# GEGLU block: sums of the down weights on GpSimd, and another order of the opening

## Chip, cores and metric

The kernel runs on one core of a Trainium2 chip. The metric is the device time of one execution in microseconds. Three runs of the kernel before took 549.56 to 552.13 us, with a median of 549.72 us.

## What is computed

The reference, cut to what matters (x is 2048 x 1024, the gate and up weights 1024 x 3584, the down weights 3584 x 1024, all bf16):

```python
def reference(x, w_gate, w_up, w_down):
    g = jnp.einsum("bsd,df->bsf", x, w_gate)
    u = jnp.einsum("bsd,df->bsf", x, w_up)
    h = _gelu(g) * u
    return jnp.einsum("bsf,fd->bsd", h, w_down)
```

## The kernel before

All three products are made by a Winograd form of Strassen's scheme: a product of 2 x 2 blocks by seven block products in place of eight, at the price of sums of blocks that are made ahead. Here `s` are sums of weight blocks and `t` sums of blocks of x; the products that use them run on TensorE in fp32r.

**Passes and units.** The 2048 rows are taken in two passes (`ip`) of 1024 rows, each as two blocks of 512 columns of the transposed x (`xT[0]`, `xT[1]`). In a pass, 14 units (`u`) each make 256 columns of h from 256 columns of both weights; then the down stage (`down`) makes the output of the pass.

**One unit** (`unit`). TensorE issues, in this order: the product of the weights' second half with `xT[0]`; s2 with t2; s1 with t1; s3 with t3; s4 with tb; the first product of the next unit (`ahead_of_p4`); sa with t4. Each of these is done for gate and up. ACT copies intermediate results out of PSUM (`snap`) and makes the gelu; VectorE adds them (`add`, `new`) and multiplies into `hT` (`times`). The last unit has no next unit's product.

**What stands beside a unit.** `prepare` runs after the s1 product has been issued. It lets GpSimd make the eight s sums of the next unit (`make_s(ahead, pool)`), has SP load the weights of the unit after the next (`load_w`, two DMAs of 512 KB, three buffers `w`), and has SP fetch the raw down weights that the next unit will need (`fetch_wd`, two DMAs of 256 KB for each j). `aside(-1)` of unit 1 issues the load of unit 2's weights on ACT's queue.

**The sums of the down weights.** For each of 14 block rows j (`NJ`) the down stage needs three sums of blocks of the down weights. The first pass makes them once and keeps them in DRAM (`td`), where the down stage of both passes loads them (`load12`, `load4`). Each j is a set: `keep(j, part)` makes one of three tensor_tensor sums on VectorE, in the tile `m` (one buffer), at the points `aside(0)`, `aside(1)`, `aside(2)` of a unit; `store_made(j)` has SP store the tile of 768 KB. `making(u)` says which j a unit makes: one each in units 2 to 12, two in units 6, 8 and 10, none in unit 13. The store of a unit's last set is issued at the head of the next unit's program.

**The down stage.** Step -1 to 2 of `down` has SP load the raw weights of the first product (`fetch12`, L305, 256 KB each; one serves two steps of four products), and after them the sums from DRAM (L266, L273). TensorE's first product of the stage reads the first of these tiles.

**The opening.** Some 8 products of zeros (`NWARM`, L460) run while x is loaded. `turn` transposes a block of x on TensorE, four tiles of 128 rows, and copies each from PSUM (L424 VectorE, L426 ACT, by turns). Unit 0 is done with plain products (`plain`): first block of x, transposed; the first half of its products; second block transposed; the second half; then the products of the second block. Its weights come in eight DMAs of 128 KB (L433). VectorE makes the s of unit 1 and the t sums of the pass in between.

**What sets the order.** SP, VectorE, GpSimd and TensorE execute in the order in which the program issues (`manual_schedule(engines=ORDER)`); ACT has its order from a scheduler, apart from the opening. Small tiles (s, t, raw, copies) share 52 slots of 2 KB per partition (`slot`); a tile gets a slot when an earlier one is released.

Helpers record most operations: L90 is every tensor_tensor on VectorE, L93 every one on GpSimd, L111 every product, L107 the copies out of PSUM, L243 the fetch of raw down weights, L256 the store of the sums, L121 the load of unit weights.

Of the kernel before, what the change touches and what calls it, by code (L numbers as in the profile page):

```python
# [10 lines left out]
def kernel(  # L11
# [23 lines left out]
    nc = tc.nc  # L35
    ENG = mybir.EngineType
    ORDER = {ENG.SP, ENG.DVE, ENG.Pool, ENG.PE}
    P = nc.NUM_PARTITIONS
    bf16 = mybir.dt.bfloat16
# [15 lines left out]
    N = 512  # L55
    NS = N // P
    NPASS = S // (2 * N)
    NU = NFB // 2
    NWARM = 8
    SLOTS = 52  # L60
    LAG = 3
    BIG12 = (0, 2, 4)
# [26 lines left out]
    def dve(out, a, b, op):  # L89
        nc.vector.tensor_tensor(out=out, in0=a, in1=b, op=op)  # L90
# [85 lines left out]
    def gelu(src):  # L176
        g = slot([P, N], f32, "g")
        nc.scalar.activation(g, src, ACT.Gelu_apprx_tanh)  # L178
        return g

    def times(fb, c, g, u):
        dve(hT[:, fb // NJ, fb % NJ, c, :], g, u, MUL)

    def product(ps, lhs, rhs, start):
        for k in range(KH):
            matmul(ps, lhs[:, k, :], rhs[k], start and k == 0, k == KH - 1)
# [6 lines left out]
    def unit(u, banks, xT, w, s, t, p1, after_p5, aside, ahead_of_p4):  # L193
        GU = range(2)

        def add(ps, other):

            g = new(dve, ps[0], other[0], ADD, "sum", dtype=f32)
            dve(ps[1], ps[1], other[1], ADD)
            return g, ps[1]  # L200

        b21 = [xT[0][:, KH + k, :] for k in range(KH)]
        e, c, d = banks
        aside(-1)
        for i in GU:
            product(c[i], w[:, i, KH:, :P], b21, True)
        g, up = add(c, p1)
        for i in GU:
            product(e[i], s["s2"][i], t["t2"], False)
        times(2 * u, 0, gelu(g), up)  # L210
        aside(0)
        u2 = [snap(e[i], "u2") for i in GU]
        c = d
        for i in GU:
            product(c[i], s["s1"][i], t["t1"], True)
        p5 = [snap(c[i], "p5") for i in GU]
        after_p5()
        for i in GU:
            product(e[i], s["s3"][i], t["t3"], False)
        g, up = new(dve, e[0], p5[0], ADD, "sum", dtype=f32), banks[1][1]  # L220
        dve(up, e[1], p5[1], ADD)
        for i in GU:
            product(c[i], s["s4"][i], t["tb"], False)
        times(2 * u + 1, 1, gelu(g), up)
        aside(1)
        g, up = add(c, u2)
        ahead_of_p4()
        for i in GU:
            product(e[i], s["sa"][i], t["t4"], False)
        times(2 * u, 1, gelu(g), up)  # L230
        aside(2)
        times(2 * u + 1, 0, gelu(e[0]), e[1])
# [9 lines left out]
        for kh in range(2):  # L242
            nc.sync.dma_start(out=wraw[j][kh], in_=wdn[:, kh, j, :])  # L243

    def keep(j, part):
        ra, rb = wraw[j]
        if part == 0:
            made[j] = mpool.tile([P, 3, N], f32r, name="m")
            dve(made[j][:, 0], ra[:, N:], ra[:, :N], SUB)
        elif part == 1:  # L250
            dve(made[j][:, 1], rb[:, N:], made[j][:, 0], SUB)
        else:
            dve(made[j][:, 2], rb[:, :N], made[j][:, 1], SUB)

    def store_made(j):
        nc.sync.dma_start(out=td[:, j], in_=made[j].bitcast(f32))  # L256

    q12, s12, q73, q4, raw = {}, {}, {}, {}, {}  # L260

# [152 lines left out]
            t.append(xn)  # L414
        return t

    def turn(xT, xn, c):
        for i in range(NS):
            tp = bank[4 + i].bitcast(bf16).rearrange("p (k r) -> p k r", k=NKB)
            for ko in range(NKB):  # L420
                nc.tensor.transpose(tp[:, ko, :], xn[i][:, ko * P : (ko + 1) * P], ident)  # L421
            dst = xT[c][:, :, i * P : (i + 1) * P]
            if i % 2 == 0:
                nc.vector.tensor_copy(out=dst, in_=tp)  # L424
            else:
                nc.scalar.copy(out=dst, in_=tp)  # L426

    xT = new_x()
    xn0 = load_x(0)
    wf = wpool.tile([P, 2, NKB, 2 * P], bf16, name="w")  # L430
    for k in range(0, NKB, 2):
        for i, src in enumerate((w_gate, w_up)):
            nc.sync.dma_start(  # L433
                out=wf[:, i, k : k + 2],
                in_=src[k * P : (k + 2) * P, 0 : 2 * P].rearrange(
                    "(ko ki) f -> ki ko f", ki=P
                ),
            )
    xn1 = load_x(1)
    w = load_w(1)  # L440
    def plain(ps, c, kos):
        for k in range(kos.start, kos.stop, 2):
            for p, (j, i) in zip(ps, [(j, i) for j in range(2) for i in range(2)]):
                for ko in (k, k + 1):
                    matmul(
                        p,
                        wf[:, i, ko, j * P : (j + 1) * P],
                        xT[c][:, ko, :],
                        ko == 0,
                        ko == NKB - 1,  # L450
                    )

    def finish(ps, c):
        for j in range(2):
            times(j, c, gelu(ps[2 * j]), ps[2 * j + 1])

    s, t = sums_s(w, dve), sums_t(xT)
    with tc.manual_schedule(engines={ENG.Activation}):
        for _ in range(NWARM):
            nc.tensor.matmul(bank[3], lhsT=warm[:, :P], rhs=warm, start=True, stop=True)  # L460
        turn(xT, xn0, 0)
        plain(bank[0:4], 0, range(0, KH))
        turn(xT, xn1, 1)
        plain(bank[0:4], 0, range(KH, NKB))
        s.make("s1", "s2")
        t.make("t1", "t2")
        finish(bank[0:4], 0)
        t.make("t3", "tb")
        s.make("s3", "sa")
        plain(bank[4:8], 1, range(NKB))  # L470
        finish(bank[4:8], 1)

    def making(u):

        steps = [[], []]
        for n in range(2, NU - 1):
            first = sum(map(len, steps))
            steps.append([first, first + 1] if n in (6, 8, 10) else [first])
        return steps[u] if u < NU - 1 else []

    nxt = {}
    ahead = None
    for ip in range(NPASS):
        for u in range(1 if ip == 0 else 0, NU):
            js = making(u) if ip == 0 else []

            def prepare():
                nonlocal ahead
                nxt["w"], nxt["s"] = ahead, None
                if u + 1 < NU:  # L490
                    nxt["s"] = make_s(ahead, pool)
                if u + 2 < NU:
                    ahead = load_w(u + 2)
                for j in making(u + 1) if ip == 0 else []:
                    fetch_wd(j)

            def aside(part):
                nonlocal ahead
                if ahead is None:
                    ahead = load_w(2, nc.scalar)  # L500
                if part == 0 and "s4" not in s:
                    s.make("s4")
                    t.make("t4")
                if part < 0:
                    return
                if len(js) == 1:
                    keep(js[0], part)
                elif js and part != 1:
                    for n in range(3):
                        keep(js[part // 2], n)  # L510
                    if part == 0:
                        store_made(js[0])

            if ip == 0 and making(u - 1):
                store_made(making(u - 1)[-1])
            def ahead_of_p4():
                if u + 1 < NU:
                    nxt["p1"] = first_product(even if u % 2 else odd, xT, nxt["w"])

            e = odd if u % 2 else even  # L520
            p1 = nxt.pop("p1", None) or first_product(e, xT, w)
            unit(u, (e, cc, dd), xT, w, s, t, p1, prepare, aside, ahead_of_p4)
            if u + 1 < NU:
                w, s = nxt["w"], nxt["s"]

        last = ip == NPASS - 1
        got, nxt = {}, {}

        def more(step):

            nonlocal ahead
            if last:
                return
            if step == 0:
                xT[:] = new_x()
            if step >= 16 and step % 2 == 0 and step // 2 - 8 < len(moves):
                c, ko = moves[step // 2 - 8]
                r0 = (2 * (ip + 1) + c) * N
                nc.sync.dma_start_transpose(
                    out=xT[c][:, ko, :], in_=x2[r0 : r0 + N, ko * P : (ko + 1) * P]  # L540
                )
            if step == 50:
                got["w"], ahead = load_w(0), load_w(1)
            if step == 58:
                got["s"] = make_s(got["w"], dve)
            if step == 62:
                got["t"] = make_t(xT)

        down(ip, even + cc, dd + odd, last, more)
        even, odd, cc, dd = odd, even, dd, cc  # L550
        if not last:
            w, t, s = got["w"], got["t"], got["s"]
# [29 lines left out]
```

## Time and profile before

| what | us |
|---|---|
| median of three runs | 549.72 |
| the profiled execution | 549.72 |
| its span, first to last instruction | 547.9 |
| busy time of TensorE (PE) | 537.1 |
| busy time of VectorE (DVE) | 361.0 |
| busy time of GpSimd (POOL) | 243.3 |
| start of unit 2 and of unit 13, first pass | 39.59, 182.03 |
| start of the first down stage | 192.63 |
| VectorE's 42 sums of down weights | 47.0 |
| GpSimd's 200 sums of unit weights | 246.0 |

The views print one row for each instruction or run of like instructions: start and duration in us, engine, line, operation, tile written and read, and in brackets the idle time of the engine before it with what ended that. PE is TensorE's products, PEld its weight loads, SPq the issues on SP's queue. An issue row shows when a DMA was issued and not when it landed; the time to landing is a view of its own. Products overlap, so their starts say more than their durations. On GpSimd and VectorE a row's duration includes a small overlap with the next.

### The profile page before, as it was taken

Reading aid. Unit: us, or ns where it says so; the run is one execution under the profiler, and the core shown is the slowest. Engines: PE = TensorE matmul, PEld = TensorE weight load, DVE = VectorE, ACT = ScalarE, POOL = GpSimd, SP = SyncE. Lnnn points to the kernel's source line nnn. Section 1 sums busy time; section 2 is a strip of 40 time slices with the busy share of each in tenths; the row PEclk is TensorE's granted clock in tenths of the full one; section 3 lists DMA queues with packets and bytes.
Section 4 is the critical chain, followed back from the end, with each engine's and each line's share of the span. In section 5 each row is a group of like instructions: output and inputs, shape, how many; then the busy total and the mean of one; then the engine's idle time right before and its main releaser. Section 6 shows DMA issues by size and latency. Waiting matters only on the chain.

```text
span 547.9 us, 7374 instructions
## 1 busy us (share of the span) xinstructions
PE 537.1 (98%) x2397; PEld 378.9 (69%) x2432; DVE 361.0 (66%) x533; ACT 243.2 (44%) x430; POOL 243.3 (44%) x206
## 2 busy tenths in 40 slices
PE   8999999999999999999999999999999999999997
PEld 4467777676767745888877776776677775478886
DVE  1897878887878697585955555545555448766730
ACT  2744555454545411155435554555455551114531
POOL 0049997495949200000077677777777600000000
PEclk9999999999999999999999999999999999999999
DMA  8291776768684699999745322222222059463751
GB/s 265 56 254 47 202 188 218 231 213 238 203 252 151 205 364 276 251 189 266 275 121 145 81 78 77 78 78 78 77 78 77 1 177 373 161 209 114 230 183 52
DMA packets 104389, 93.28 MB, mean 170 GB/s; under 512 B 12960, under 2 KB 88736, under 8 KB 104352
## 3 DMA queue, kind: packets, MB, share of 16 engines
q1 hardware_dynamic: 102272, 91.77, 56.1%
q10 hardware_dynamic: 2080, 1.05, 0.7%
q8 instruction: 19, 0.31, 0.2%
q14 instruction: 18, 0.15, 0.1%
HBM read 75.50 MB, written 15.20 MB: 166 GB/s over the span
## 4 chain that ended last, share of the span: by engine, by line
PE 88%; DMA 6%; DVE 4%; issue 1%; ACT 1%; SPq 1%; ACTq 0%; DVEq 0%
PE bank L111 88%; DMA td<-m 4%; DVE m L90 3%; DMA xn<-in_x_dram 1%; DMA w<-in_w_gate_dram 1%; SPq L413 1%; DVE hT L90 0%; ACT g L178 0%; DVE sum L90 0%; ACT u L107 0%; PE bank L421 0%; ACT st L384 0%; ACT p L107 0%; DVEq L90 0%; ACTq L107 0%
## 5 line engine op out<-in xcount | busy, mean ns | idle before, releaser
L93 POOL TENSOR_TENSOR s<-w 128x512 fp32r<-128x512 bf16 x100 | 124.0, 1259 | 193.2 <-DVE t L90 95.7
L111 PE MATMUL bank<-t,s 128*128 128x512 f32 x648 | 157.9, 398 | 2.4 <-ACT u L107 2.4
L111 PEld LDWEIGHTS bank<-t,s 128*128 128x128 f32 x648 | 121.5, 188 | 31.2 <-issue 2.2
L111 PE MATMUL bank<-xT,w 128*128 128x512 bf16 x467 | 110.5, 380 | 3.0 <-ACT xT L426 1.1
L107 ACT COPY p<-bank 128x512 f32<-128x512 f32 x124 | 70.5, 590 | 77.8 <-PE bank L111 65.2
L90 DVE TENSOR_TENSOR hT<-g,bank 128x512 bf16<-128x512 f32 x112 | 76.5, 686 | 37.0 <-ACT g L178 30.1
L178 ACT ACTIVATE g<-sum 128x512 f32<-128x512 f32 x81 | 51.2, 633 | 96.7 <-DVE sum L90 95.7
L111 PEld LDWEIGHTS <-w 128*128 128x128 bf16 x496 | 44.3, 98 | 60.6 <-issue 14.3
L90 DVE TENSOR_TENSOR sum<-bank,p 128x512 f32<-128x512 f32 x54 | 37.1, 686 | 55.5 <-PE bank L111 49.4
L93 POOL TENSOR_TENSOR s<-w,s 128x512 fp32r<-128x512 bf16 x50 | 63.9, 1298 | 0.0
L111 PE MATMUL bank<-q 128*128 128x512 f32 x240 | 58.9, 389 | 0.0
L111 PE MATMUL bank<-t,sa 128*128 128x512 f32 x216 | 58.5, 412 | 0.0
L93 POOL TENSOR_TENSOR s<-s,w 128x512 fp32r<-128x512 f32 x50 | 58.1, 1182 | 0.0
L111 PE MATMUL bank<-tb,s 128*128 128x512 f32 x216 | 53.4, 389 | 0.0
L111 PEld LDWEIGHTS bank<-q 128*128 128x128 f32 x240 | 45.1, 188 | 9.3
L111 PE MATMUL bank<-raw,hT 128*128 128x512 bf16 x218 | 48.4, 379 | 0.3
L111 PEld LDWEIGHTS bank<-t,sa 128*128 128x128 f32 x216 | 40.5, 188 | 11.3 <-DVE sum L90 1.0
L111 PEld LDWEIGHTS bank<-tb,s 128*128 128x128 f32 x216 | 40.6, 188 | 8.5
L102 ACT CAST tb<-raw 128x512 fp32r<-128x512 bf16 x28 | 17.2, 626 | 58.8 <-PE bank L111 24.1
L90 DVE TENSOR_TENSOR q<-hT 128x512 fp32r<-128x512 bf16 x56 | 38.4, 686 | 6.1 <-PE bank L111 6.1
L107 ACT COPY u<-bank 128x512 f32<-128x512 f32 x62 | 34.6, 586 | 16.8 <-PE bank L111 16.6
L90 DVE TENSOR_TENSOR bank<-bank,p 128x512 f32<-128x512 f32 x54 | 37.4, 693 | 4.4 <-PE bank L111 3.2
(42 smaller groups left out, 445.8 us busy)
## 6 DMA issues: line engine op xcount, KB each, us to landing
raw<-in_w_down_dram SPq DMA_DIRECT2D x84, 256.0 KB, 5.0
q<-td SPq DMA_DIRECT2D x60, 256.0 KB, 4.9
w<-in_w_gate_dram SPq DMA_DIRECT2D x26, 512.0 KB, 5.2
w<-in_w_up_dram SPq DMA_DIRECT2D x26, 512.0 KB, 6.2
td<-m SPq DMA_DIRECT2D x14, 768.0 KB, 4.5
w<-td SPq DMA_DIRECT2D x6, 1024.0 KB, 9.3
out_dram<-st SPq DMA_DIRECT2D x32, 128.0 KB, 1.7
xn<-in_x_dram SPq DMA_DIRECT2D x8, 256.0 KB, 4.8
```

The costliest lines, as they stand in the source:

```text
L90: nc.vector.tensor_tensor(out=out, in0=a, in1=b, op=op)
L93: nc.gpsimd.tensor_tensor(out=out, in0=a, in1=b, op=op)
L102: nc.scalar.copy(out=t, in_=src)
L107: nc.scalar.copy(out=t, in_=ps)
L111: nc.tensor.matmul(ps, lhsT=lhs, rhs=rhs, start=start, stop=stop, skip_group_check=True)
L178: nc.scalar.activation(g, src, ACT.Gelu_apprx_tanh)
L413: nc.sync.dma_start(out=xn, in_=x2[r0 : r0 + P, :])
```

## The change

There are three parts.

1. `keep` makes all three sums of a set on GpSimd, in one go, and has SP store them at once. It is called in `prepare`, after GpSimd's s sums of the next unit and after the load of unit weights, and ahead of the fetch of the next raw weights. `store_made` is gone. `making` gives one set to each of units 2 to 12 (j = u - 2) and three, 11 to 13, to unit 13; the second and third of those take a buffer of the unit weights (`wpool`) for their tile.
2. In a unit `aside(0)` comes ahead of the first `times`. Only unit 1 has work there now: VectorE's s4 and t4 sums.
3. In the opening there are 5 products of zeros in place of 8; three of the first block's four copies are VectorE's; unit 0's weights come in three pairs of DMAs (2, 3 and 3 blocks) in place of four; the first products are issued on half the columns at a time; the transposes of the second block stand in two pairs between the later products; t1 and s1 are made first, then the first gelu products, then t2 and s2.

```diff
-    NWARM = 8
+    NWARM = 5
...
+        aside(0)
         times(2 * u, 0, gelu(g), up)
-        aside(0)
...
-    def keep(j, part):
+    def keep(j, spare):
         ra, rb = wraw[j]
-        if part == 0:
-            made[j] = mpool.tile([P, 3, N], f32r, name="m")
-            dve(made[j][:, 0], ra[:, N:], ra[:, :N], SUB)
-        elif part == 1:
-            dve(made[j][:, 1], rb[:, N:], made[j][:, 0], SUB)
+        if spare:
+            m = wpool.tile([P, 4, N], f32r, name="w")
         else:
-            dve(made[j][:, 2], rb[:, :N], made[j][:, 1], SUB)
-
-    def store_made(j):
-        nc.sync.dma_start(out=td[:, j], in_=made[j].bitcast(f32))
+            m = mpool.tile([P, 3, N], f32r, name="m")
+        pool(m[:, 0], ra[:, N:], ra[:, :N], SUB)
+        pool(m[:, 1], rb[:, N:], m[:, 0], SUB)
+        pool(m[:, 2], rb[:, :N], m[:, 1], SUB)
+        nc.sync.dma_start(out=td[:, j], in_=m[:, :3].bitcast(f32))
...
-    for k in range(0, NKB, 2):
+    for k0, k1 in ((0, 2), (2, 5), (5, NKB)):
...
+    def plain(ps, c, kos, parts=1):
+        n = N // parts
         for k in range(kos.start, kos.stop, 2):
+            for part in range(parts):
+                cols = slice(part * n, (part + 1) * n)
...
-        turn(xT, xn0, 0)
-        plain(bank[0:4], 0, range(0, KH))
-        turn(xT, xn1, 1)
-        plain(bank[0:4], 0, range(KH, NKB))
-        s.make("s1", "s2")
-        t.make("t1", "t2")
+        for i in range(NS):
+            turn(xT, xn0, 0, i, on_act if i == 1 else on_dve)
+        plain(bank[0:4], 0, range(0, 2), parts=2)
+        plain(bank[0:4], 0, range(2, 4))
+        for i in range(2):
+            turn(xT, xn1, 1, i, on_act if i % 2 else on_dve)
+        plain(bank[0:4], 0, range(4, 6))
+        for i in range(2, NS):
+            turn(xT, xn1, 1, i, on_act if i % 2 else on_dve)
+        plain(bank[0:4], 0, range(6, NKB))
+        t.make("t1")
+        s.make("s1")
         finish(bank[0:4], 0)
+        t.make("t2")
+        s.make("s2")
         t.make("t3", "tb")
         s.make("s3", "sa")
...
     def making(u):
-        steps = [[], []]
-        for n in range(2, NU - 1):
-            first = sum(map(len, steps))
-            steps.append([first, first + 1] if n in (6, 8, 10) else [first])
-        return steps[u] if u < NU - 1 else []
+        if u < 2 or u >= NU:
+            return []
+        return list(range(u - 2, NJ if u == NU - 1 else u - 1))
...
                 if u + 2 < NU:
                     ahead = load_w(u + 2)
+                for j in js:
+                    keep(j, j != js[0])
                 for j in making(u + 1) if ip == 0 else []:
                     fetch_wd(j)
...
-                if part < 0:
-                    return
-                if len(js) == 1:
-                    keep(js[0], part)
-                elif js and part != 1:
-                    for n in range(3):
-                        keep(js[part // 2], n)
-                    if part == 0:
-                        store_made(js[0])
-
-            if ip == 0 and making(u - 1):
-                store_made(making(u - 1)[-1])
```

More of the change, by code (lines that the diff above doesn't have):

```diff
@@ L415, in load_x, with turn @@
         return t
[L417 to L426, printed above, removed]
+    def turn(xT, xn, c, i, copy):
+        tp = bank[4 + i].bitcast(bf16).rearrange("p (k r) -> p k r", k=NKB)
+        for ko in range(NKB):
+            nc.tensor.transpose(tp[:, ko, :], xn[i][:, ko * P : (ko + 1) * P], ident)
+        copy(out=xT[c][:, :, i * P : (i + 1) * P], in_=tp)
     xT = new_x()
@@ L430 @@
     wf = wpool.tile([P, 2, NKB, 2 * P], bf16, name="w")
-    for k in range(0, NKB, 2):
+    for k0, k1 in ((0, 2), (2, 5), (5, NKB)):
         for i, src in enumerate((w_gate, w_up)):
             nc.sync.dma_start(
-                out=wf[:, i, k : k + 2],
-                in_=src[k * P : (k + 2) * P, 0 : 2 * P].rearrange(
+                out=wf[:, i, k0:k1],
+                in_=src[k0 * P : k1 * P, 0 : 2 * P].rearrange(
                     "(ko ki) f -> ki ko f", ki=P
@@ L440 @@
     w = load_w(1)
-    def plain(ps, c, kos):
+    def plain(ps, c, kos, parts=1):
+        n = N // parts
         for k in range(kos.start, kos.stop, 2):
[L443 to L451, printed above, removed]
+            for part in range(parts):
+                cols = slice(part * n, (part + 1) * n)
+                for p, (j, i) in zip(ps, [(j, i) for j in range(2) for i in range(2)]):
+                    for ko in (k, k + 1):
+                        matmul(
+                            p[:, cols],
+                            wf[:, i, ko, j * P : (j + 1) * P],
+                            xT[c][:, ko, cols],
+                            ko == 0 and part == 0,
+                            ko == NKB - 1,
+                        )
     def finish(ps, c):
@@ L455, in finish @@
             times(j, c, gelu(ps[2 * j]), ps[2 * j + 1])
+    on_dve, on_act = nc.vector.tensor_copy, nc.scalar.copy
     s, t = sums_s(w, dve), sums_t(xT)
```

## The prediction

> **What bounds the kernel now.** I read the engine line first: PE is busy 98% of the span, so a change can win only PE's holes or open new ones. The profiled execution took 549.72 us, which is also the median of the three timed runs, with a span of 547.9 us; I work in span time and add 1.8 us.
>
> ```profile
> PE 537.1 (98%) x2397; PEld 378.9 (69%) x2432; DVE 361.0 (66%) x533; ACT 243.2 (44%) x430; POOL 243.3 (44%) x206
> ```
>
> Then PE's timeline of the first pass (start, duration).
>
> ```profile
> 39.59 1.67 PE L111 MATMUL bank<-xT,w 128*128 128x512 bf16 x7
> ...
> 52.19 1.67 PE L111 MATMUL bank<-xT,w 128*128 128x512 bf16 x7
> ...
> 129.96 4.00 PE L111 MATMUL bank<-t,s 128*128 128x512 f32 x16
> 135.06 2.08 PE L111 MATMUL bank<-t,s 128*128 128x512 f32 x8 [1.10 <-ACT u L107]
> ...
> 182.03 1.67 PE L111 MATMUL bank<-xT,w 128*128 128x512 bf16 x7
> ...
> 192.63 22.62 PE L111 MATMUL bank<-raw,hT 128*128 128x512 bf16 x101
> ```
>
> An undisturbed unit lasts 52.19 - 39.59 = 12.60 us. From unit 2 (39.59) to unit 13 (182.03) PE needs 142.44 us; eleven clean units are 138.60. The 3.84 us between are holes in units 6 to 10, where two m sets in one unit make VectorE late. The last unit takes 10.60 us and the down stage starts at 192.63.
>
> Third, GpSimd and VectorE, side by side.
>
> ```profile
> 44.84 2.28 POOL L93 TENSOR_TENSOR s<-w 128x512 fp32r<-128x512 bf16 x2
> 47.09 2.28 POOL L93 TENSOR_TENSOR s<-s,w 128x512 fp32r<-128x512 f32 x2
> 49.33 2.73 POOL L93 TENSOR_TENSOR s<-w 128x512 fp32r<-128x512 bf16 x2
> 52.02 2.75 POOL L93 TENSOR_TENSOR s<-w,s 128x512 fp32r<-128x512 bf16 x2
> 54.73 2.28 POOL L93 TENSOR_TENSOR s<-w 128x512 fp32r<-128x512 bf16 x2
> ```
> ```profile
> 302.09 2.29 POOL L93 TENSOR_TENSOR s<-w 128x512 fp32r<-128x512 bf16 x2 [3.56 <-PE bank L111]
> 304.34 2.28 POOL L93 TENSOR_TENSOR s<-s,w 128x512 fp32r<-128x512 f32 x2
> 306.57 2.28 POOL L93 TENSOR_TENSOR s<-w 128x512 fp32r<-128x512 bf16 x2
> 308.81 2.31 POOL L93 TENSOR_TENSOR s<-w,s 128x512 fp32r<-128x512 bf16 x2
> ```
> ```profile
> 95.79 3.13 DVE L90 TENSOR_TENSOR m<-raw,m 128x512 fp32r<-128x512 bf16 x2
> ...
> 104.29 1.42 DVE L90 TENSOR_TENSOR m<-raw,m 128x512 fp32r<-128x512 bf16 x2
> ```
>
> A pair of s sums starts 2.24 us after the one before (302.09, 304.34), so one costs 1.12 us. In the first pass some pairs take 2.73, exactly where VectorE works on m at the same time (48.35 and 52.08), and an m pair on VectorE takes 3.13 us beside GpSimd and 1.42 while GpSimd is idle. Sums and products that read PSUM do not do this: the second pass has the same ones and no slow pair. So a set of eight s costs 9.0 us alone (302.09 to 311.12) and 9.9 beside m (44.84 to 54.73).
>
> Last, SP's queue where the first pass ends.
>
> ```profile
> 171.54 11.46 SPq L256 DMA_DIRECT2D td<-m  x2
> 183.11 3.17 SPq L305 DMA_DIRECT2D raw<-in_w_down_dram  x5
> ```
>
> SP issues in program order. The second of these stores waits for the last m sum (VectorE, until 182.6), and the weights of the down stage (L305) are issued only behind it, at 183.11. The first lands 4.64 us later, at 187.75, 4.9 us before PE wants it. This place decides my forecast.
>
> **The sums move to GpSimd.** VectorE loses 42 sums (30.2 + 16.8 = 47 us of its busy time) and its waits for the m buffer; that removes the 3.84 us of holes. GpSimd gains 42 sums, three in each of units 2 to 12 and nine in unit 13. No m sum ran on GpSimd, so the nearest rows are its s sums, 1.12 us. The second and third m sum each read the one before at once; on VectorE that adds 0.73 - 0.60 = 0.13 us (103.56 to 104.29 against 0.60 between independent ones). I take 0.1 each: 3.6 us for a set, 3.4 if nothing is added, 4.0 at the high end. A GpSimd unit is then 9.0 + 3.6 = 12.6 us, as long as PE's 12.60: GpSimd has no slack, but does not fall behind either. Its s are in time: in this trace s(3) begins at 44.84, and with my sums the s that PE wants at 1.3 us into a unit is ready some 4 us before.
>
> The Trainium skill, GPSIMD Engine Reference, section 4.1, speaks against the move: elementwise work with two inputs belongs on VectorE, GpSimd being about twice as slow. By that, an estimate of 2 x 0.69 = 1.38 us a sum would make a GpSimd unit 13.1 us and the forecast some 8 us longer; the rows here show 1.12, so I do not use it.
>
> **When GpSimd is done.** GpSimd's chain starts with s(2) at 34.46, when w(2) lands (issued by ACT at 26.97, 7.4 us to landing). s(2) ended at 44.87, one of its sums beside an m sum, so now 44.4. Then s(3), 53.4; the set m(0), 57.0; ten more GpSimd units at 12.6: 183.0. That is the end of m(10), in unit 12's program, and SP's store of it goes then. SP fetches the raw weights of sets 11, 12 and 13 behind this store (six DMAs of 256 KB). The rows have the same sequence once: the store at 182.68, the first 256 KB behind it landed at 187.75, 5.1 us later. So m(11) begins at 188.1, and three sets end at 188.1 + 3 x 3.6 = 198.9. PE, without holes, would finish the units at 39.59 + 11 x 12.60 + 10.60 = 188.8.
>
> **What is late next.** The store of set 13 now waits on SP until 198.9, and behind it, in order, stand all loads of the down stage: L305 first, then the td loads. Again 5.1 us from store to the first landing: 204.0. PE's first down product reads that tile, so it starts at 204.0 in place of 192.63. The fetch and the three sets have no cover: PE has nothing else left, since the last unit issues no product ahead. From there the down stage runs as before (355.3 us to the end of the span); its later loads follow at the old distances, some 0.3 us late at the ninth tile (201.96 - 187.75 = 14.2 us behind the first, wanted 16 x 0.86 = 13.8 behind it).
>
> After such a wait PE may be slow. The rows show this only at the opening: warm-up products 0.43 us apart and later ones 0.21, slow until about 5.2 us, some 2.0 us lost. The longest hole later, 1.10 us, is followed by full speed. So nothing to 2.0 us; I take 1.0. The Trainium skill, TensorE: Matmul & The Clock Gate, Part 1, gives a half-rate clock after an idle window of about 3.4 us, which no row of this trace reaches; by it half of a further 3.4 us, an estimate of 1.7 us, would be lost.
>
> **The opening.** Three warm-ups go (3 x 0.43 us), under a wait for x that ends at about 4 us. The last copy of x goes from ACT (1.01 us) to VectorE (0.69). The first product waited until 8.43 for that copy; half-width products need only the first two, and the first weights (7.47), so PE starts some 0.9 us earlier. The transposes of x's second block waited 0.63 + 0.21 + 0.21 + 0.26 = 1.3 us for DMAs; products now stand between them, and six weight DMAs in place of eight bring SP to those x loads about 1 us earlier. At best 1.9 us is won. Against it, fewer warm-ups may leave the first 16 products (3.4 us) at half speed, which would turn the gain into a loss of up to 1.0. I take 1.0 us won; all times above shift by it, GpSimd's chain included, since w(2)'s issue follows PE. The new order of t and s sums on VectorE changes no end: the same sums are due at 28.3, where PE first reads t2 and s2, and VectorE is through them some 2 us before. In unit 1, t4 and s4 (4.75 us) now go ahead of one hT product that only the down stage reads: nothing.
>
> **Sum.** 204.0 - 1.0 = 203.0 against 192.63: 10.4 us later. With 1.0 for the slow restart and 0.3 for the loads, 549.72 + 11.7 = 561.4 us, say **561**. The 3.84 us of holes are won and then waited away.
>
> **Rivals.** (1) **Faster, 544.9 us, chance 0.08.** The loads of the down stage are not held: 549.72 - 3.84 - 1.0. For it: VectorE's lateness is the only thing that holes PE today. It decides if GpSimd's last sum ends by 182.7 (187.8 less 5.1), 15 us before my sum; against it stands the row at 183.11. (2) **GpSimd keeps its slow pace, 579 us, chance 0.07.** If its sums stay at 9.9 and 4.1 us a unit for a reason other than m on VectorE, units 2 to 12 take 14.0, its last fetch lands at 221.4 - 1.0, and the total is 27.8 + 1.3 us above. The second pass speaks against it. (3) **Half and half, 550 us, chance 0.06.** w(2) lands as fast as L305's fastest load (2.6 us, not 7.4) and the six raw pieces no longer wait behind a store (another 5 us), so that holes won and wait pay each other. (4) My case, 0.79.
>
> **The numbers.** In case 4 the low end is: sets of 3.4 us (14 of them, 2.8), an opening of 1.9 (0.9), no slow restart (1.0), first load in 2.6 us (2.0): 554.7. The high end is sets of 4.0 (5.6), the opening lost (2.0), the slow restart in full (1.0): 570. Rival 3 pulls the low end to 551; both highest terms at once are unlikely, so 569. Under 0.5% (2.7 us) a measurement of this kernel cannot tell from no change. Faster 0.08; within, 0.04 (rival 3 mostly); slower 0.88.
>
> **What would show it.** GpSimd's timeline without gaps from 33 to about 182 us and sums at 1.12 us apart; unit starts 12.60 us apart throughout; then a gap of some 15 us on PE before its first raw,hT product, ended by a DMA of L305; SP's store standing until GpSimd's last m sum. I am wrong if the L305 loads are issued before the last store, if GpSimd's m sums cost far from 1.2 us, or if holes open inside the units.

## The result, and the profile after

The changed kernel takes 563.77 us (median of four runs, 562.3 to 564.37) against 549.64 us for the kernel before on the same chip: ratio 1.0246, 95% interval 1.0207 to 1.0284. It is slower by 14 us; 561.0 was predicted, in a range of 551 to 569. The profiled execution took 563.86 us, with a span of 561.9.

The engine line of the page after, to be held against the one of before:

```profile
PE 541.4 (96%) x2402; PEld 382.1 (68%) x2437; DVE 320.5 (57%) x492; ACT 245.8 (44%) x429; POOL 279.2 (50%) x248
```

VectorE is 40 us less busy and GpSimd 36 us more, and PE has lost its 98%. Where, PE's timeline shows (start, duration, and in brackets the idle time before the row and what ended it):

```profile
38.31 1.67 PE L111 MATMUL bank<-xT,w 128*128 128x512 bf16 x7
...
176.91 1.67 PE L111 MATMUL bank<-xT,w 128*128 128x512 bf16 x7
178.24 4.00 PE L111 MATMUL bank<-t,s 128*128 128x512 f32 x16
183.27 1.20 PE L111 MATMUL bank<-t,s 128*128 128x512 f32 x4 [1.04 <-ACT u L107]
...
189.57 2.08 PE L111 MATMUL bank<-t,s 128*128 128x512 f32 x4 [5.10 <-ACT u L107]
192.06 3.78 PE L111 MATMUL bank<-tb,s 128*128 128x512 f32 x8 [0.42 <-ACT p L107]
195.65 2.23 PE L111 MATMUL bank<-t,sa 128*128 128x512 f32 x8
203.82 1.01 PE L111 MATMUL bank<-raw,hT 128*128 128x512 bf16 x2 [5.95 <-DMA raw<-in_w_down_dram]
```

- Unit 2 starts 1.28 us earlier than before, and the eleven units to 176.91 take 138.60 us, 12.60 each: the 3.84 us of holes are gone. At unit 13 the kernel is 5.1 us ahead.
- Unit 13, which took 10.60 us, now takes some 21 and ends at about 197.9. Holes of 1.04, 5.10 and 0.42 us are 6.6 us of that; the other 4 us, nearly, are slow products behind the long hole (the granted clock is 0.50 from 186 to 196 us).
- Then PE idles 5.95 us for the first down tile. The down stage begins at 203.82 in place of 192.63: 11.2 us later.
- From there to the end of the span it takes 561.9 - 203.82 = 358.1 us, where it took 355.3.

GpSimd's timeline, a unit in the middle and the end of the pass:

```profile
55.33 2.28 POOL L93 TENSOR_TENSOR s<-w 128x512 fp32r<-128x512 bf16 x2
...
64.30 1.16 POOL L93 TENSOR_TENSOR m<-raw 128x512 fp32r<-128x512 bf16 x1
65.54 2.43 POOL L93 TENSOR_TENSOR m<-raw,m 128x512 fp32r<-128x512 bf16 x2
68.04 2.29 POOL L93 TENSOR_TENSOR s<-w 128x512 fp32r<-128x512 bf16 x2
...
187.75 1.15 POOL L93 TENSOR_TENSOR m<-raw 128x512 fp32r<-128x512 bf16 x1 [5.15 <-DMA raw<-in_w_down_dram]
...
196.19 2.40 POOL L93 TENSOR_TENSOR w<-raw,w 128x512 fp32r<-128x512 bf16 x2
```

A GpSimd unit lasts 68.04 - 55.33 = 12.71 us, as long as PE's; a set costs 68.04 - 64.30 = 3.74. In unit 13 GpSimd first waits 5.15 us for the raw weights, then makes three sets. SP's queue beside it:

```profile
182.63 0.33 SPq L254 DMA_DIRECT2D td<-m  x1
183.05 3.42 SPq L243 DMA_DIRECT2D raw<-in_w_down_dram  x6
191.42 0.33 SPq L254 DMA_DIRECT2D td<-m  x1
195.02 3.92 SPq L254 DMA_DIRECT2D td<-w  x2
199.04 3.14 SPq L301 DMA_DIRECT2D raw<-in_w_down_dram  x5
```

Three stores wait here, each for its set; the last goes at about 198.6, and only behind it the first down weights (L301 is L305 of before). They land at 203.78, and PE's product follows at 203.82.

What made the holes in unit 13 is in ACT's waits (170 to 206 us: total, times, longest) and ACT's timeline:

```profile
ACT u L107 <- POOL m L93: 7.6, 2, 5.7
```
```profile
188.93 0.59 ACT L107 COPY u<-bank 128x512 f32<-128x512 f32 x1 [5.71 <-POOL m L93]
```

`u` is a copy out of PSUM that reads nothing of `m`. What it needs besides is one of the 52 small slots, and the raw weights of sets 11 to 13 hold their slots until GpSimd's m sums have read them. That the slot is what it waits for is inferred from the code; the trace names GpSimd's sum and not the slot. This was not in the prediction; here it lies beneath the wait for the down tile.

### The profile page after: what moved, and what is told of

It reads as the page before. It is cut to its first block, busy times and chain, and to the rows that moved or that the text cites. A ratio compares the mean times of both kernels' runs of the same rounds, so it can differ in the third digit from the quotient of the medians.

```text
span 561.9 us, 7351 instructions
## 1 busy us (share of the span) xinstructions
PE 541.4 (96%) x2402; PEld 382.1 (68%) x2437; DVE 320.5 (57%) x492; ACT 245.8 (44%) x429; POOL 279.2 (50%) x248
## 4 chain that ended last, share of the span: by engine, by line
PE 89%; DMA 3%; POOL 3%; DVE 2%; issue 1%; ACT 0%; SPq 0%; POOLq 0%; DVEq 0%
PE bank L111 89%; DMA raw<-in_w_down_dram 2%; POOL m L93 1%; DVE t L90 1%; POOL w L93 1%; DMA xn<-in_x_dram 1%; POOL s L93 1%; DVE s L90 1%; PE bank L416 0%; DVE hT L90 0%; SPq L409 0%; ACT xT L417 0%; DVE sum L90 0%; SPq L254 0%; ACT g L178 0%
## 5 line engine op out<-in xcount | busy, mean ns | idle before, releaser
L93 POOL TENSOR_TENSOR s<-w 128x512 fp32r<-128x512 bf16 x100 | 118.4, 1205 | 164.1 <-DVE t L90 92.5
L111 PE MATMUL bank<-xT,w 128*128 128x512 bf16 (+1 forms) x475 | 110.9, 376 | 1.9
L93 POOL TENSOR_TENSOR s<-w,s 128x512 fp32r<-128x512 bf16 x50 | 57.7, 1175 | 0.0
L111 PE MATMUL bank<-raw,hT 128*128 128x512 bf16 x218 | 51.1, 394 | 6.4 <-DMA raw<-in_w_down_dram 5.9
L111 PE MATMUL bank<-tb,s 128*128 128x512 f32 x216 | 55.1, 399 | 0.4 <-ACT p L107 0.4
L111 PEld LDWEIGHTS <-hT 128*128 128x128 bf16 x224 | 22.5, 101 | 34.8 <-issue 10.4
```

The lines of the kernel that those rows point to most:

```text
L93: nc.gpsimd.tensor_tensor(out=out, in0=a, in1=b, op=op)
L111: nc.tensor.matmul(ps, lhsT=lhs, rhs=rhs, start=start, stop=stop, skip_group_check=True)
```

## The experiments

The theory: SP issues in order, so the down weights stand behind the stores of sets 11 to 13, and these behind GpSimd, which has no time for the three sets before PE is done. Its rivals: the time is lost to the slots (the holes in unit 13), to the slow restart, to GpSimd's pace, or to the opening. All times are medians; each ratio is to the kernel before on the same chip.

**1. The opening alone (x_open).** Part 3 of the change without parts 1 and 2.

```diff
-    NWARM = 8
+    NWARM = 5
...
+    def turn(xT, xn, c, i, copy):
...
+    def plain(ps, c, kos, parts=1):
...
+        plain(bank[0:4], 0, range(0, 2), parts=2)
```

This diff is to the kernel before; `keep` stays on VectorE and `aside(0)` behind `times`.

> The kernel before with the new opening alone; the sums of the down weights stay on VectorE. Theory (the opening is worth 1.3 us and all of the loss comes from the sums): unit 2 starts at 38.3, the 3.8 us of holes in units 6 to 10 stay, the down stage starts at about 191.3, total 548.4 us. Rival (the opening shares in the loss, for instance by cold products): unit 2 at 39.6 or later and 550 us or more.

551.38 us, ratio 1.0049 (1.003 to 1.0067): a miss by 3 us, where 1.3 us were to be won. VectorE's timeline, then PE's:

```profile
32.03 5.38 DVE L90 TENSOR_TENSOR t<-xT,t 128x512 fp32r<-128x512 bf16 x4
```
```profile
38.06 2.11 PE L111 MATMUL bank<-t,sa 128*128 128x512 f32 x8 [1.69 <-DVE sum L90]
40.24 1.67 PE L111 MATMUL bank<-xT,w 128*128 128x512 bf16 x7
```

The four t4 sums of unit 1 take 5.38 us here, beside GpSimd's s sums, and the sum that PE waits for stands behind them on VectorE. In the kernel before they took 3.46 us: they began at 33.19, 1.3 us ahead of GpSimd (34.46). The new opening brings GpSimd 2.2 us forward (32.29) and t4 only 1.2, so that they overlap more. The same row in the kernel before, and then in the changed kernel:

```profile
33.19 3.46 DVE L90 TENSOR_TENSOR t<-xT,t 128x512 fp32r<-128x512 bf16 x4
```
```profile
31.27 2.49 DVE L90 TENSOR_TENSOR t<-xT,t 128x512 fp32r<-128x512 bf16 x4
```

With `aside(0)` ahead of `times` they begin 1.0 us ahead of GpSimd's first sum (32.25), and GpSimd gives way: its first pair takes 3.65 us. The head start alone does not decide which engine gives way, as x_split2 shows below.

**2. The opening with the new order of aside (x_open2).** As x_open, with s4 and t4 made ahead of the first `times`, as part 2 has it; VectorE's m sums keep their place behind it (`aside(0)`). This diff is to x_open.

```diff
+        aside(-2)
         times(2 * u, 0, gelu(g), up)
         aside(0)
...
-                if part == 0 and "s4" not in s:
+                if part == -2 and "s4" not in s:
```

> The kernel before with the new opening and the new order of s4 and t4 in unit 1; the sums of the down weights stay on VectorE. Theory (the opening's gain is kept only if t4 is through before GpSimd's s sums begin): unit 2 starts at 38.3 and not at 40.2 as in x_open, the holes of units 6 to 10 stay, total 550 - 1.3 = 548.5 us. Rival (the opening gains nothing either way): 550 us or more.

548.34 us, ratio 0.9962 (0.9947 to 0.9976), as expected. Unit 2 starts at 38.93 in this profile and the down stage at 191.83; the holes of the kernel before are still there (in units 7 to 11, as they are in its trace). The opening wins its time only together with the order of `aside`.

**3. Loads ahead of the stores (x_defer).** The stores of sets 11 to 13 are issued in the down stage, behind its first four loads.

```diff
-        nc.sync.dma_start(out=td[:, j], in_=m[:, :3].bitcast(f32))
+        made[j] = m
+        if j < 11:
+            put(j)
...
         def step(n):
+            if ip == 0 and n == 1:
+                for j in range(11, NJ):
+                    put(j)
```

`put(j)` issues the store that stood in `keep`.

> The changed kernel, with the stores of sets 11 to 13 issued on SP behind the first four loads of the down stage. Theory (those loads wait on SP for the stores): they are issued at about 186.5, right behind the raw fetches, TensorE goes from unit 13 into the down stage without a gap at about 197.9 (unit 13 keeps its holes of 6.6 us), and the slow restart goes as well: 563.8 - 5.9 - 2.8 = 555 us. Rival (the end of the sums itself sets the down stage, not SP's order): 563.8 us.

563.08 us, ratio 1.0257 (1.0238 to 1.0276): nothing won, which is the rival's number. Its queue on SP and PE's timeline:

```profile
183.26 3.42 SPq L243 DMA_DIRECT2D raw<-in_w_down_dram  x6
196.33 1.92 SPq L306 DMA_DIRECT2D raw<-in_w_down_dram  x4
```
```profile
199.09 7.07 PE L111 MATMUL bank<-raw,hT 128*128 128x512 bf16 x31 [1.89 <-DMA raw<-in_w_down_dram]
...
208.94 1.89 PE L111 MATMUL bank<-raw,hT 128*128 128x512 bf16 x8 [2.78 <-DMA raw<-in_w_down_dram]
```

No store stands between the two SP rows, and yet SP waits until 196.33. That is when GpSimd's first sum of set 13 ends (195.14 + 1.16 = 196.30) and gives back a raw slot. The down tile needs a slot too, and reads nothing else of GpSimd's, so the slot is what it most likely waited for. PE starts 4.7 us earlier, but the later tiles and sums are late in turn; in five holes from 195 to 225 us it waits 8.1 us.

**4. The raw weights fetched earlier (x_fetch).** In `prepare` the fetch goes ahead of `keep`, so that it no longer stands behind a store.

```diff
+                for j in making(u + 1) if ip == 0 else []:
+                    fetch_wd(j)
                 for j in js:
                     keep(j, j != js[0])
-                for j in making(u + 1) if ip == 0 else []:
-                    fetch_wd(j)
```

> The changed kernel, with the fetch of the next raw weights issued on SP ahead of the sums and of the store that waits for them. Theory (GpSimd waits 5.15 us for raw 11 because its fetch stands behind the store of set 10): that wait goes, the last sum ends at about 193.5, the first down product starts at 198.7, total 558.7 us. Rival (raw tiles fetched earlier hold slots that ACT's copies need): new holes inside the units, 563 us or more.

563.05 us, ratio 1.0255 (1.0236 to 1.0275): again nothing. That is the rival's number, but not for its reason, since no new holes open. The wait of 5.15 us for raw weights is gone, and so are the holes in unit 13. In its place GpSimd waits for the one m buffer, whose store must land; and the last sums now fall beside VectorE's sums of the down stage and are slow:

```profile
186.24 1.16 POOL L93 TENSOR_TENSOR m<-raw 128x512 fp32r<-128x512 bf16 x1 [3.43 <-DMA td<-m]
...
195.78 3.05 POOL L93 TENSOR_TENSOR w<-raw,w 128x512 fp32r<-128x512 bf16 x2
```
```profile
204.07 1.01 PE L111 MATMUL bank<-raw,hT 128*128 128x512 bf16 x2 [14.83 <-DMA raw<-in_w_down_dram]
```

The gap of 15 us that the prediction named is here in one piece, since unit 13 is clean and ends at 189.2. The down stage starts when it did. So the holes in unit 13 cost the changed kernel nothing: they were hidden beneath the wait behind the last store, which goes at 198.85 here. Why the earlier fetch frees unit 13 of its holes, though the raw tiles then hold their slots for longer, was not followed up.

**5. Loads before the last two units' work (x_early).** The first four down loads are issued in unit 12, ahead of the store of set 10; the down stage then leaves them out.

```diff
...
+                if ip == 0 and u == NU - 2:
+                    for n in range(4):
+                        fetch12(n)
                 for j in js:
                     keep(j, j != js[0])
```

> The changed kernel, with the first four loads of the down stage issued in unit 12, ahead of the store of set 10, so that neither the last stores on SP nor a slot held by raw weights can hold them. Theory (both of these waits held the down stage's first tile, the stores until 198.6 and the slot until 196.3): TensorE goes from unit 13, which keeps its holes, into the down stage at about 198 and at full speed, the fifth load lands at about 204.5 just in time: 563.4 - 5.9 - 2.8 = 554.7 us. Rival (four more tiles take slots from unit 13, which grows by as much, or the later loads hole the down stage as in x_defer): 560 us or more.

560.12 us, ratio 1.0183 (1.0157 to 1.0208); 5 us more than expected, and in the rival's range. PE's timeline:

```profile
194.91 3.46 PE L111 MATMUL bank<-t,s 128*128 128x512 f32 x8 [8.12 <-ACT u L107]
...
201.85 13.99 PE L111 MATMUL bank<-raw,hT 128*128 128x512 bf16 x62
```

No wait is left at the head of the down stage, but four more tiles hold slots, and the hole in unit 13 grows to 8.12 us. ACT waits there for m sums that it does not read (5.4 us before copies, 7.6 before gelus). What was hidden is now the path: unit 13 itself ends at 201.85.

**6. Products of zeros in the gap (x_warm).** PE is kept busy while it waits; nothing reads the result.

```diff
         step(-1)
+        if ip == 0:
+            for _ in range(24):
+                nc.tensor.matmul(c[0], lhsT=warm[:, :P], rhs=warm,
+                                 start=True, stop=True)
```

> The changed kernel, with 24 products of zeros on TensorE between unit 13 and the down stage. They compute nothing that is used. Theory (the first 14 down products start 0.43 us apart because TensorE stood idle for 5.95 us): the zeros take up the wait, the down products start at 203.8 and 0.22 us apart, total 563.4 - 2.8 = 560.6 us. Rival (the slow products have another cause, such as late loads): 563.4 us, products still 0.43 us apart.

561.47 us, ratio 1.0206 (1.0181 to 1.023), 2.3 us less than the changed kernel, whose ratio on its own chip is 1.0246. Both kernels' windows over the first 3.2 us of the down stage (stretch, us, busy time of PE, PEld, DVE, ACT, POOL, granted clock, DMA share, GB/s), after and then x_warm:

```profile
203.80:207.00 3.20, 2.95 (x7) 1.13 (x8) 3.13 (x6) 0.00 (x0) 0.00 (x0) 0.50 1.05 358
```
```profile
203.80:207.00 3.20, 2.58 (x12) 1.17 (x12) 3.10 (x6) 0.00 (x0) 0.00 (x0) 1.00 1.07 346
```

Seven products against twelve (x_warm starts 0.6 us later in this window, at 204.42), at a granted clock of 0.50 against 1.00. In x_warm the rest of the span is 559.6 - 204.42 = 355.2 us, that of before. So the whole 2.8 us after the start is the slow restart, and the later loads cost nothing.

**7. Three sets left out (x_leave).** Sets 11 to 13 are not made and not stored, and the down stage reads set 10 in their place. That part of the output isn't the reference's.

```diff
     def making(u):
...
-        return list(range(u - 2, NJ if u == NU - 1 else u - 1))
+        return [u - 2] if u < NU - 1 else []
...
-                nc.sync.dma_start(out=q, in_=td[:, j, n])
+                nc.sync.dma_start(out=q, in_=td[:, min(j, 10), n])
...
-        nc.sync.dma_start(out=q, in_=td[:, j, 2])
+        nc.sync.dma_start(out=q, in_=td[:, min(j, 10), 2])
```

> The changed kernel, with sets 11 to 13 left out: GpSimd makes sets 0 to 10 in units 2 to 12 and none in unit 13, and the down stage reads set 10 in place of the three. Theory (all of the loss, and both waits at the head of the down stage, come from the three sets in unit 13): the store of set 10 is issued at 182.6, the first load of the down stage lands at 187.7, when TensorE ends unit 13 (187.5), no hole, full speed: 549.6 - 4.9 = 544.8 us. Rival (the eleven sets on GpSimd cost something as well): 547 us or more.

546.41 us, ratio 0.993 (0.9911 to 0.9949), between the theory and the rival. SP's queue and PE's timeline, with unit 2 at 39.96 in this profile:

```profile
184.23 0.33 SPq L254 DMA_DIRECT2D td<-m  x1
184.65 3.13 SPq L301 DMA_DIRECT2D raw<-in_w_down_dram  x5
```
```profile
187.35 1.98 PE L111 MATMUL bank<-t,sa 128*128 128x512 f32 x8
189.40 5.77 PE L111 MATMUL bank<-raw,hT 128*128 128x512 bf16 x25
```

Without the three sets all is gone: the wait but for some 0.2 us, the holes in unit 13, the slow restart. The eleven sets that stay cost PE nothing in the units (39.96 to 178.56 are 138.60 us). What the change loses, it loses in unit 13.

**8. All sets on GpSimd, none in unit 13 (x_spread).** The second sets go to units 6, 8 and 10, as before.

```diff
     def making(u):
...
-        return list(range(u - 2, NJ if u == NU - 1 else u - 1))
+        steps = [[], []]
+        for n in range(2, NU - 1):
+            first = sum(map(len, steps))
+            steps.append([first, first + 1] if n in (6, 8, 10) else [first])
+        return steps[u] if u < NU - 1 else []
...
-                    keep(j, j != js[0])
+                    keep(j, False)
```

> The changed kernel, with all 14 sets on GpSimd but spread as in the kernel before: two in units 6, 8 and 10, none in unit 13, all through the one m buffer. Theory (GpSimd's unit of 12.7 us has no room beside TensorE's 12.6): each second set costs GpSimd its 3.6 us and a wait of some 3.4 us for the store of the first, 21 us in all; 4 us are in hand, so unit 13 starts about 17 us late, the last store goes at about 203.6, the down stage starts at about 208.7, and the total is 566 to 568 us. Rival (it was only the place of the last sets): 546 to 553 us.

567.61 us, ratio 1.0317 (1.0301 to 1.0333), as expected. A unit with two sets is GpSimd's, 9.0 + 7.4 us and a wait for the m buffer, against 12.6 of PE:

```profile
109.69 1.15 POOL L93 TENSOR_TENSOR m<-raw 128x512 fp32r<-128x512 bf16 x1 [3.45 <-DMA td<-m]
```
```profile
197.03 1.67 PE L111 MATMUL bank<-xT,w 128*128 128x512 bf16 x7
...
209.67 22.65 PE L111 MATMUL bank<-raw,hT 128*128 128x512 bf16 x101 [1.88 <-DMA raw<-in_w_down_dram]
```

Unit 13 starts 20 us later than in the changed kernel: GpSimd has no slack in units 6, 8 and 10 either.

**9. The sets divided (x_split).** On x_open: VectorE makes one set in each of units 2 to 12, GpSimd the other three, in units 5, 8 and 11; two m buffers, 49 slots. GpSimd's store of such a set is issued two units later.

```diff
+    EXTRA = {5: 11, 8: 12, 11: 13}
     def making(u):
-        steps = [[], []]
...
-        return steps[u] if u < NU - 1 else []
+        return [u - 2] if 2 <= u < NU - 1 else []
...
+                if ip == 0 and u in EXTRA:
+                    keep_pool(EXTRA[u])
```

> The new opening; VectorE makes one set in each of units 2 to 12, GpSimd sets 11 to 13 in units 5, 8 and 11, with a second m buffer (paid for with 3 of the 52 slots); no set in unit 13. Theory (the loss comes only from where the last sets are made, the holes of the kernel before only from two sets in one unit): no holes in the units, the down stage starts at about 187.5 and runs at full speed, 549.6 - 3.8 - 1.3 = 544.5 us. Rival (49 slots are too few, or VectorE and GpSimd slow each other into new holes): 548 us or more.

551.25 us, ratio 1.0035 (1.0017 to 1.0053): a miss by 7 us, again in unit 1. PE's timeline, in an execution of 553.04 us, the longest of ten:

```profile
41.40 3.78 PE L111 MATMUL bank<-t,sa 128*128 128x512 f32 x8 [3.54 <-DVE sum L90]
45.43 2.55 PE L111 MATMUL bank<-xT,w 128*128 128x512 bf16 x7 [0.24 <-issue]
```

It has the old order of `aside`; t4 takes 6.32 us beside GpSimd, which began 2.3 us ahead of it, and the hole is 3.54 us, with slow products behind it. After that no hole is left up to the down stage, which starts at 195.53.

**10. The same with s4 and t4 early (x_split2).** In unit 1 they are made ahead of `times`.

```diff
+        aside(-2)
         times(2 * u, 0, gelu(g), up)
...
-                if part == 0 and "s4" not in s:
+                if part == -2 and "s4" not in s:
                     s.make("s4")
                     t.make("t4")
```

> As x_split, and in unit 1 VectorE makes s4 and t4 ahead of its first hT product, as the changed kernel does. Theory (x_split lost its gain in unit 1: t4 came beside GpSimd's s sums, TensorE had a hole of 3.54 us and then ran slowly, so that unit 2 started at 45.4 and not at 38.3; from there on it had no hole): unit 2 starts at about 38.3, the down stage at about 187.5, total 544.5 us. Rival (the order of these six sums is worth nothing, as I predicted): 551 us.

**545.29 us, ratio 0.9915 (0.9894 to 0.9935)**: faster than both kernels.

```profile
38.40 1.67 PE L111 MATMUL bank<-xT,w 128*128 128x512 bf16 x7
...
176.99 1.67 PE L111 MATMUL bank<-xT,w 128*128 128x512 bf16 x7
...
187.60 24.35 PE L111 MATMUL bank<-raw,hT 128*128 128x512 bf16 x109
```

It keeps what the changed kernel wins (unit 2 at 38.40, no holes to 176.99) and starts the down stage at 187.60, 5.0 us before the kernel before and 16.2 before the changed one. In unit 1 GpSimd's first pair and the t4 sums read:

```profile
30.85 5.12 POOL L93 TENSOR_TENSOR s<-w 128x512 fp32r<-128x512 bf16 x2 [29.54 <-DMA w<-in_w_gate_dram]
```
```profile
31.34 2.49 DVE L90 TENSOR_TENSOR t<-xT,t 128x512 fp32r<-128x512 bf16 x4
```

GpSimd begins 0.5 us ahead of t4 here, and yet t4 keeps its pace and GpSimd's pair is the slow one.

**11. The same with eight products of zeros (x_split3).** `NWARM = 8` on x_split2.

> As x_split2, with 8 products of zeros in the opening in place of 5. Theory (x's later tiles land at 5.3 to 7.0 us in every run, so three more products cost nothing, and they keep TensorE busy through its slow start): as x_split2 or up to 1 us less, with less spread between runs; 544 us. Rival (they delay the transposes): 0.5 to 1.3 us more than x_split2.

545.52 us, ratio 0.9916 (0.9894 to 0.9937): no difference from x_split2. Unit 2 starts at 38.62.

## Why the prediction was right

The mechanism is the one on record. By its steps:

- **GpSimd's pace.** Predicted 3.6 us a set and 12.6 a unit; measured 3.74 and 12.71, with no slow pair in units 2 to 12. m(10)'s store was put at 182.0 (183.0 less the opening) and went at 182.63. Two small errors partly cancel there: GpSimd began at 32.25 and not at 33.46, and needed 150.4 us from there to the end of m(10) in place of 148.5.
- **The fetch and the three sets.** 5.1 us from store to m(11): m(11) predicted at 187.1, began at 187.75. The last set predicted to end at 197.9; its store went at 198.6.
- **The down tile behind the store.** First down product predicted at 203.0, seen at 203.82. x_leave shows that the three sets are the whole cause: without them the stage starts straight behind unit 13, at 189.40.
- **The rival "faster", 544.9 us,** had the right price: x_split2, another kernel, where the loads are not held, takes 545.29.
- **GpSimd's slow pace** did not come in the units. It came in x_fetch (3.05 us a pair), under the condition that was named: VectorE's sums of SBUF data beside it.

What was wrong:

- **The slow restart was mis-sized.** With the later loads it was taken at 1.3 us, and the bound for the restart was 2.0; together they cost 2.8, and x_warm shows that the restart is all of it. The bound came from the opening of one trace, where fewer products were slow. This term is 1.5 us of the 2.5 by which the working (561.4) was below the profiled 563.86; the later start of the stage is 0.8, and the time around the span (1.96 in place of 1.8) the rest.
- **"Nothing" for the order of t4 and s4 was wrong.** The prediction asked only when the product behind them was needed, and not what GpSimd does at that time. With the old order t4 loses its pace beside GpSimd's first sums, with the new one it keeps it: the opening alone loses 2.2 us (551.38 against 549.14 on its chip), with the order it wins 1.9 (548.34 against 550.25 on its own). In the changed kernel's profile the two parts gave 1.28 where 1.0 was taken for one of them: the sum came out near by luck. Other profiles with the same opening and order have unit 2 at 38.40 to 39.96, against 39.59 in the kernel before.
- **The holes in unit 13 were not foreseen.** "PE, without holes, would finish the units" was an assumption; PE finished some 10 us later (197.9 against 187.8). That cost the changed kernel nothing, as x_fetch shows, but it is one of the signs that the prediction named for being wrong ("if holes open inside the units"), it makes the last gap 5.95 us in place of some 15, and it is why x_early wins only 3.7 us (563.77 - 560.12; by the ratios, 1.0183 against 1.0246), and the slots, as far as the code tells, are why x_defer wins nothing.
- **The holes of 3.84 us were misplaced by a unit.** In the trace of the kernel before they stand in units 7 to 11 (102.59 to 169.43), and not in 6 to 10. Their sum is right, and nothing else in the forecast hangs on the place.

At the head of the down stage three bounds lie close together: SP's store (198.6), the raw slots that GpSimd holds (196.3 in x_defer), and unit 13's own end (197.9; 201.85 in x_early). The parts of the slots in the second and third are inferred. Taking one away uncovers the next; of the edits tried, only leaving the three sets out, or giving eleven of the fourteen back to VectorE, removes all three. A version with more than 52 slots was not tried.

The Trainium skill, GPSIMD Engine Reference, section 4.1, was set aside in the prediction because twice 0.69 us would be 1.38 a sum. The rows agree with it better than that: VectorE's four t4 sums take 2.49 us together in the changed kernel, the last of them 0.69, so they start 0.60 us apart; twice that is 1.20, against 1.12 measured on GpSimd. The error was to double a duration that includes overlap.

## What to carry to other kernels

Before moving work to an idle engine, fill in that engine's unit against the unit of the engine that bounds: here 12.7 against 12.6 us leaves no place for three more sets, and what does not fit piles up in the last unit. Then follow the in-order queue and the buffers behind the late work, since a store that waits holds back all loads behind it, and inputs that wait hold slots that others need; freeing one of them is worth nothing while another stands just below. Dividing the work, eleven sets on the engine that had room and three on the other, gave the gain that moving all of it could not.

## What the runs showed of the hardware

- **An idle PE comes back slow, and for longer than the opening suggested.** After 5.95 us without products, fourteen were 0.43 us apart (203.82 to 209.75), at a granted clock of 0.50 in the first 3.2 us. Holes of 3.54 us (x_split), 3.69 and 3.98 us (x_spread) and 5.10 us (unit 13 of the changed kernel) were followed by slow products as well; after 2.78 us (x_defer, eight products in 1.89) the pace was full. The time back to full pace differs: 5.9 us here, 4.1 us in x_fetch (nine products at a granted clock of 0.50 from 204.07 to 208.2, then 1.00), 2.9 us in x_early (seven at 0.50 from 194.91 to 197.86, then 1.00). The Trainium skill, TensorE: Matmul & The Clock Gate, Part 1, puts both the idle time that sets half rate and the busy time that lifts it at about 3.4 us, and has that time counted in windows that run on without regard to the kernel. The first agrees with these holes. For the second, the spread from 2.9 to 5.9 us can come from where in a window the products resume: in the changed kernel the half rate lasts from 203.0 to 209.8 us, twice 3.4. The 2.9 us are still shorter than one window, which no run here explains.
- **Which of two engines gives way can change, and not simply by which starts first.** Four t4 sums on VectorE took 2.49 us in the changed kernel, where they began 1.0 us ahead of GpSimd's sums, whose first pair then took 3.65, and 5.38 in x_open, where they began 0.3 us ahead. But they took 2.49 as well in x_split2, where they began 0.5 us behind GpSimd, and with the same 1.3 us ahead they took 3.46 in the kernel before and 2.49 in x_open2. With s4 and t4 ahead of the first product into hT VectorE kept its pace in every profile, with the old order (the kernel before, x_open, x_split) in none; why is not shown. The Trainium skill, GPSIMD Engine Reference, section 1, names contention between GpSimd and VectorE instructions with two SBUF inputs; these rows agree, and add that the price falls on either side.
- **The start varies.** With the same five products of zeros and the new order unit 2 began at 38.31 to 39.96 in different profiles; in x_leave (39.96) 23 half-width products of the opening took 4.70 us and in the changed kernel 3.78. Some of it is that x lands later (the first of these products starts at 7.98 us there, and at 7.08 in the changed kernel), and the rest that PE comes to full pace later: the first 2.1 us of them hold 12 products in x_leave, and the first 1.9 us hold 20 in the changed kernel. What brings the full pace late was not settled; eight products of zeros (x_split3) made no difference in the medians.
